# Stores of the first pass on GpSimd's queue, grouped matmuls, and half-size temporaries in an attention and two-MoE kernel

## The chip, the core and the metric

The kernel runs on one core of one Trainium2 chip. The metric is the time of one execution on the device in microseconds (us). Before the change three runs took 1383.2, 1383.8 and 1381.34 us, a median of 1383.2. All rows below are of one profiled execution of 1381.88 us.

The core has five engines with their own instruction rows: TensorE (PE, its weight loads shown as PEld), VectorE (DVE), ScalarE (ACT), GpSimd (POOL) and SyncE (SP). An engine takes its instructions in the order in which they are written and waits at each until its inputs and its output buffer are ready. A transfer (DMA) is an instruction of the engine that starts it; it then runs by itself.

## The reference

Attention between x (8 batches, 8 heads, 512 positions, 64 wide) and a state (32 positions), in both directions; the result is 4352 tokens of width 512. Two MoE layers follow, each with one weight pair 512 x 2048 and 2048 x 512, the first with a squared ReLU, the second with SiLU.

```
scores  = scale * x @ state^T;   xread = softmax(scores) @ state
scores2 = scale * state @ x^T;   sread = softmax(scores2) @ x
x = concat(xread, sread) as 4352 tokens of 512
h = relu(x @ w_in);  x = (h * h) @ w_out
h = x @ w_in2;       out = (h * sigmoid(h)) @ w_out2
```

## The kernel before

**Numbers.** Every product is made from pairs: a value is split into hi and lo in fp32r and three (in the last product two, the second on half the width) matmuls are added up. The weights come as 64-bit words and are converted on the chip: a transfer brings the raw words of a block into a page, ScalarE takes a first step (c_abs), VectorE three or four more (c_bits, c_sum or c_split).

**Buffers.** Nearly all data lie in 50 pages of 128 x 1024 fp32 and 10 quads of 128 x 512 (pools of rotating buffers). The eight banks of PSUM are four pairs: psA, psB, psC, psD.

**Stages.** The first layer does not multiply x by w1 for the part that comes from the state: it forms G = state x w1 (g_unit, line 579), four small 64 x 64 matmuls in fp32 for a group, two groups for a unit, 16 units in two halves. A group writes two banks; each bank is copied out into a page go (by ScalarE or VectorE), and from there some parts go to other pages (Glo) through small transfers, the rest to DRAM (g_d) and back later. The converted w1 is also stored (w1_store, line 604). Then the first pass runs: gemm1 into psC, ScalarE and VectorE make the squared ReLU (rg, gact), gemm2 adds into psA and psB. The scores of the attention (scores, line 641) go into psD between those. For each token block evac_a (line 820) writes sums of the result to DRAM (x_d). The second layer is two products (gemm3, gemm4) that each use seven half-size products in place of eight, with temporaries U, R, W and X in gemm4 (line 1034): U is copied from psA by ScalarE, then VectorE adds a bank to it block by block, and join (line 1060) adds the two halves of a temporary into the result z.

**The order.** A planner (class Plan) records all operations with what they read and write, gives each an urgency, and lists them in order per engine by modelled costs (cost, line 107; record, 142; urgency, 190; order, 220). An operation recorded with `either` may go to one of two engines; arith (line 451) chooses between VectorE and GpSimd, copy (line 455) between ScalarE and VectorE. All instructions are issued by one helper in record, so the profile shows line 186 for all of them (188 in the changed kernel); the buffers' names tell them apart. Before the change every transfer is SyncE's, through 8 lanes.

Of the kernel before, what the change touches and what calls it, by code (L numbers as in the profile page):

```python
# [27 lines left out]
class Plan:  # L28
# [6 lines left out]
    LATENCY = dict(act=dict(act=153, dve=147, pool=159, pe=265, dma=0),  # L35
                   dve=dict(act=128, dve=127, pool=155, pe=256, dma=0),
                   pool=dict(act=150, dve=150, pool=150, pe=309, dma=0),
                   pe=dict(act=197, dve=196, pool=200, pe=3, dma=0),
                   dma=dict(act=0, dve=0, pool=0, pe=100, dma=0))
    LANES = 8  # L40
    WINDOW = 25
# [9 lines left out]
    def __init__(self, bufs):  # L51
        self.bufs = bufs
        self.ops = []
        self.tiles = {}
        self.seen = {}
        self.slot = 0

# [49 lines left out]
    def cost(self, eng, method, writes, reads, args):  # L107
        size = 1
        for ap in writes + reads:
            n = 1  # L110
# [4 lines left out]
        if eng == "dma":  # L115
            n = 1
            for d in writes[0].shape:
                n *= d
            return n * 4 / 360
        if eng == "pe":  # L120
            n = 1
            for d in writes[0].shape[1:]:
                n *= d
            if method == "transpose":
                return 109

            share = 128 * 128 // (reads[0].shape[0] * writes[0].shape[0]) if args.get("tile_position") else 1
            return max(n / 2.4 + 13, 109) * (4 if args["rhs"].dtype == F32 else 1) / share
# [13 lines left out]
    def record(self, calls):  # L142
# [45 lines left out]
        self.ops.append(dict(forms=forms, deps=deps, uses=uses, slot=self.slot, port=port))  # L188

    def urgency(self, when=None):  # L190
# [3 lines left out]
        for i, o in enumerate(ops):  # L194
            if o["forms"][0][0] == "dma":
                cost[i] += self.LEAD
        late, t = [], 0.0
        for i, o in enumerate(ops):
            if o["forms"][0][0] == "pe":
                t = when[i] + cost[i] if when else t + cost[i]  # L200
                late.append(t)
            else:
                late.append(t + (self.DSLACK if o["forms"][0][0] == "dma" else self.SLACK))
# [16 lines left out]
    def order(self, when=None):  # L220
# [26 lines left out]
        ready = {e: [] for e in now}  # L247
# [8 lines left out]
        lanes, hw, wire = [], 0.0, 0.0  # L256
        port = dict(dve=0.0, pool=0.0)
        head = 0
        busy, warm = deque(), False

# [3 lines left out]
        def earliest(i, eng):  # L264
            o = ops[i]
            e = now[eng]
# [16 lines left out]
            if eng == "dma":  # L283
                e = max(e, hw)
                if len(lanes) >= self.LANES:
                    e = max(e, lanes[-self.LANES])
# [3 lines left out]
        while done < n:  # L290
# [4 lines left out]
            for eng, cand in ready.items():  # L295
                mine = []
                low = None
                for _, i in cand[:60]:
                    if ops[i]["slot"] > limit:
                        continue  # L300
                    e = earliest(i, eng)
# [8 lines left out]
                    if e <= now[eng] + self.PATIENCE[eng]:  # L310
                        break
                for e, i in mine:
                    if e <= low + self.PATIENCE[eng]:
# [16 lines left out]
            if eng == "pe":  # L330
# [4 lines left out]
                end[i] = now[eng] = e + cost * (1 if warm else 2)  # L335
                if busy and e - busy[-1][1] < 10:
                    busy[-1][1] = end[i]
# [12 lines left out]
            for t in o["uses"]:  # L350
                users_left[t] -= 1
                seems = e + self.DMA_SEEMS if eng == "dma" else end[i]
# [10 lines left out]
    def best(self):  # L363
        when, found = None, None
        for _ in range(self.ROUNDS):
# [12 lines left out]
def attn_moe_moe_kernel(  # L378
# [35 lines left out]
    T, D = plan.engine("pe", nc.tensor), plan.engine("dma", nc.sync)  # L414
# [115 lines left out]
    def c_store(key, dst):  # L530
        D.dma_start(dst, cv[key].rearrange("p (k n) -> p k n", k=2))
# [47 lines left out]
    def g_unit(i):  # L579
# [61 lines left out]
    def scores(b, g):  # L641
# [178 lines left out]
    def evac_a(s, j, n):  # L820
# [16 lines left out]
        for i in SEQ:  # L837
            at(s + 1, "dma", lambda i=i: D.dma_start(x_d[(i, j)].rearrange("(k p) n -> p k n", p=P), v[SRC_B[i]]))
# [195 lines left out]
    def gemm4(q):  # L1034
# [40 lines left out]
        U = new("U4")  # L1075
        for b in range(c):
            A.copy(U[:, b], BA[b])
# [14 lines left out]
        X = new("X4")  # L1092
# [143 lines left out]
    base = A_END + 2  # L1236
    for u in range(NU):
# [60 lines left out]
```

## Time and profile before

| | |
|---|---|
| runs | 1383.2, 1383.8, 1381.34 us |
| profiled execution | 1381.88 us, span 1380.1 us, mean granted clock 0.996 |
| PE busy | 1335.8 us, 97% of the span, 6892 matmuls |
| DVE busy | 1056.3 us, 77%, 1598 instructions |
| ACT busy | 701.0 us, 51%, 1080 instructions |
| POOL busy | 48.9 us, 4%, 41 instructions |
| DMA | 283.08 MB, mean 205 GB/s, one queue at 61.4% of 16 engines |

The share of an engine is a mean over the whole span and hides the stages: the first 100 us are conversion of weights and the first half of G, 140 to 160 us hold the second half of G, 160 to 960 us the first pass and gemm3, the rest ends with gemm4. A row of a timeline has the start, the duration of the row's instructions together (x2, x8 count them), and in brackets how long the engine was idle just before and what ended that.

### The profile page before, as it was taken

The numbers are of one execution on the slowest core, as the hardware profiler recorded it, in microseconds if no ns is written. First come the engines' busy times: TensorE is split into PE (matmuls) and PEld (weight loads), VectorE is DVE, ScalarE is ACT, GpSimd is POOL, SyncE is SP. The second block draws the span as 40 slices with busy tenths as digits, with TensorE's granted clock in tenths as the row PEclk, the third lists the DMA queues.
The fourth block names the chain that finished last, engine by engine and source line by source line (L and its number), as shares of the span: only waits on it lengthen the run. The fifth ranks groups of instructions, "written<-read, shape, count | busy, mean of one in ns | idle before, by whom it ended". The sixth has DMA issues, their size and how long they took to land. (4 is left out here: it accounts for less than half of the span.)

```text
span 1380.1 us, 19261 instructions
## 1 busy us (share of the span) xinstructions
PE 1335.8 (97%) x6892; PEld 1107.9 (80%) x6892; DVE 1056.3 (77%) x1598; ACT 701.0 (51%) x1080; POOL 48.9 (4%) x41
## 2 busy tenths in 40 slices
PE   5889999999999999999999999999998999999998
PEld 1457588888888888888988888999787888888887
DVE  6979488878898888875898866777887676665664
ACT  5755776555555646554662434244455444344442
POOL 0000001110000000000020000000111000000000
PEclk9999999999999999999999999999999999999999
DMA  8761764436264546342759956667899666665663
GB/s 302 262 244 62 223 219 131 123 120 216 80 198 127 168 144 194 112 153 107 225 177 328 363 208 233 248 233 255 280 338 362 195 215 231 220 204 187 201 205 114
DMA packets 206959, 283.08 MB, mean 205 GB/s; under 512 B 13456, under 2 KB 148112, under 8 KB 206864
## 3 DMA queue, kind: packets, MB, share of 16 engines
q1 hardware_dynamic: 206864, 281.86, 61.4%
q8 instruction: 54, 0.88, 0.3%
q14 instruction: 41, 0.34, 0.1%
HBM read 161.35 MB, written 116.26 MB: 201 GB/s over the span
## 5 line engine op out<-in xcount | busy, mean ns | idle before, releaser
L186 ACT ACTIVATE rg<-psC 128x512 f32<-128x512 f32 (+1 forms) x144 | 82.6, 574 | 199.0 <-PE psC L186 195.6
L186 PE MATMUL psC<-AThi,Ghi 128*128 128x512 f32 x256 | 101.6, 400 | 6.0 <-ACT rg L186 3.1
L186 DVE TENSOR_TENSOR gact<-rg,gact 128x512 fp32r<-128x512 f32 (+1 forms) x139 | 90.9, 656 | 19.0 <-ACT rg L186 12.8
L186 PE MATMUL psC<-ATlo,Ghi 128*128 128x512 f32 x256 | 101.1, 398 | 2.2 <-DVE ATlo L186 2.2
L186 PE MATMUL psC<-AThi,Glo 128*128 128x512 f32 x256 | 101.1, 399 | 1.7 <-DVE Glo L186 1.7
L186 ACT ACTIVATE gact<-rg 128x512 fp32r<-128x512 f32 (+1 forms) x144 | 87.7, 609 | 6.9 <-DMA g<-go 3.4
L186 DVE TENSOR_TENSOR rg<-rg 128x512 f32<-128x512 f32 (+1 forms) x66 | 43.7, 662 | 48.4 <-ACT rg L186 48.0
L186 PEld LDWEIGHTS psC<-AThi,Ghi 128*128 128x128 f32 x256 | 48.1, 188 | 21.4 <-ACT AThi L186 4.6
L186 DVE TENSOR_TENSOR W<-psD,U 128x512 f32<-128x512 f32 (+2 forms) x57 | 35.4, 631 | 35.9 <-PE psD L186 35.8
L186 PEld LDWEIGHTS psC<-AThi,Glo 128*128 128x128 f32 x256 | 48.0, 188 | 16.2 <-issue 3.3
L186 PEld LDWEIGHTS psC<-ATlo,Ghi 128*128 128x128 f32 x256 | 48.2, 189 | 14.8 <-DVE ATlo L186 2.9
L186 ACT ACTIVATE r<-r 128x1024 f32<-128x1024 f32 (+2 forms) x20 | 18.6, 932 | 73.3 <-DVE r L186 61.8
L186 DVE TENSOR_SCALAR cv<-cv 128x1024 f32<-128x1024 f32 (+1 forms) x64 | 43.4, 686 | 8.2 <-ACT cv L186 7.9
L186 ACT ACTIVATE rg<-rg 128x512 f32<-128x512 f32 (+1 forms) x78 | 46.3, 594 | 0.0
L186 DVE TENSOR_TENSOR U<-psB,U 128x512 f32<-128x512 f32 (+2 forms) x57 | 35.0, 629 | 14.1 <-PE psB L186 12.6
L186 DVE TENSOR_TENSOR W<-psC,U 128x512 f32<-128x512 f32 (+2 forms) x40 | 24.2, 609 | 27.6 <-PE psC L186 27.2
L186 ACT ACTIVATE cv<-raw 128x512 f32<-128x512 f32 x64 | 40.7, 668 | 8.9 <-DMA raw<-in_w_dram 8.9
L186 PE MATMUL psA<-cc,st 64*64 64x512 f32 x128 | 25.9, 641 | 17.7 <-DVE cc L186 17.3
L186 DVE SCALAR_TENSOR_TENSOR cc<-raw,cv 128x512 int32<-128x512 int32 x64 | 41.9, 684 | 1.4 <-DMA g<-go 1.2
L186 DVE SCALAR_TENSOR_TENSOR cv<-raw,cv 128x512 f32<-128x512 uint32 x64 | 41.5, 682 | 0.2
L186 DVE TENSOR_TENSOR Glo<-Glo,Ghi 128x1024 fp32r<-128x1024 f32 x31 | 37.7, 1216 | 1.2 <-ACT Ghi L186 1.0
L186 ACT COPY U<-psA 128x512 f32<-128x512 f32 (+2 forms) x57 | 28.9, 538 | 14.9 <-PE psA L186 14.3
(1244 smaller groups left out, 4276.2 us busy)
## 6 DMA issues: line engine op xcount, KB each, us to landing
raw<-in_w_dram SPq DMA_DIRECT2D x64, 512.0 KB, 6.4
t<-s SPq DMA_DIRECT2D x36, 512.0 KB, 5.0
Glo<-g SPq DMA_DIRECT2D x96, 128.0 KB, 4.6
t<-r SPq DMA_DIRECT2D x24, 512.0 KB, 4.6
xTr<-in_xT_dram SPq DMA_DIRECT2D x16, 512.0 KB, 8.3
g<-go SPq DMA_DIRECT2D x16, 512.0 KB, 5.7
xnr<-in_xN_dram SPq DMA_DIRECT2D x16, 512.0 KB, 5.6
x<-yt SPq DMA_DIRECT2D x32, 256.0 KB, 4.0
```

The source lines that it names most:

```text
L186: lambda engine=engine, method=method, a=a, k=k: getattr(engine, method)(*a, **k)))
```

## The change

Four parts. The stores c_store, w1_store, those of G to g_d and those of evac_a to x_d are started by GpSimd and not by SyncE: 119 transfers. The planner gets a second kind of transfer for them ("sdma"), on GpSimd's time with 1000 ns each. In the first pass arith goes to VectorE alone (18 operations that stood on GpSimd), and the bank copies of the first half of G go to ScalarE alone. The four matmuls of a group of G, or of a group of scores, are placed next to each other. In gemm4 U, R, W and X are quads, one for each block of 128 tokens, in place of pages for two blocks, and a join is made per block.

```diff
+    DMA = ("dma", "sdma")
     LANES = 8
+    ISSUE = 1000
     WINDOW = 25
...
-
-            share = 128 * 128 // (reads[0].shape[0] * writes[0].shape[0]) if args.get("tile_position") else 1
-            return max(n / 2.4 + 13, 109) * (4 if args["rhs"].dtype == F32 else 1) / share
+            return max(n / 2.4 + 13, 109) * (4 if args["rhs"].dtype == F32 else 1)
...
+            if o["group"] is not None:
+                cost[i] /= len(self.members[o["group"]])
...
+                    g = ops[i]["group"]
+                    if g is not None and i not in rest:
+                        if any(left[m] for m in self.members[g]):
+                            continue
+                        e = max(earliest(m, eng) for m in self.members[g])
+                    else:
...
-            elif eng == "dma":
-                hw = e + 450
-                now[eng] = e + 60
-                wire = max(wire, e + 1100) + cost
+            elif eng in self.DMA:
+                issue = 450 if eng == "dma" else self.ISSUE
+                hw[eng] = e + issue
+                now[clock[eng]] = e + (60 if eng == "dma" else issue)
+                wire = max(wire, e + 650 + issue) + cost
                 end[i] = wire + 1500
-                lanes.append(end[i])
+                lanes[eng].append(end[i])
...
-    T, D = plan.engine("pe", nc.tensor), plan.engine("dma", nc.sync)
+    T = plan.engine("pe", nc.tensor)
+
+    D, DS = plan.engine("dma", nc.sync), plan.engine("sdma", nc.gpsimd)
...
+    pool_stores = [True]
+
     def arith(op, o, a, b):
         kw = dict(out=o, in0=a, in1=b, op=op)
-        plan.either((V, "tensor_tensor", kw), (G, "tensor_tensor", kw))
+        if pool_stores[0]:
+            V.tensor_tensor(**kw)
+        else:
+            plan.either((V, "tensor_tensor", kw), (G, "tensor_tensor", kw))
 
...
-        D.dma_start(dst, cv[key].rearrange("p (k n) -> p k n", k=2))
+        DS.dma_start(dst, cv[key].rearrange("p (k n) -> p k n", k=2))
...
             ts = [acc_tile(bp), acc_tile(bp + 1)]
+            plan.together = ("G", i, bp)
             for k in range(2):
                 for r in range(2):
                     ps, co = slice(r * 64, (r + 1) * 64), 64 * (r ^ k)
                     T.matmul(out=ts[k][co:co + 64], lhsT=st[ps, bp + k, p].rearrange("p e n -> p (e n)"),
                              rhs=pg[ps], start=True, stop=True, tile_position=(r * 64, co))
+            plan.together = None
             o2 = page(f"go{i}{bp}", F32).rearrange("p (k f) -> p k f", k=2)
             for k in range(2):
-                copy(o2[:, k], ts[k])
+                (A.copy if 4 * q < PARTS[0][1] else copy)(o2[:, k], ts[k])
...
-                D.dma_start(g_d[q][0][p], o2[:, 1])
+                DS.dma_start(g_d[q][0][p], o2[:, 1])
             else:
-                D.dma_start(g_d[q][1][p], o2)
+                DS.dma_start(g_d[q][1][p], o2)
 
     def w1_store(i):
-        D.dma_start(w1_d[i], w1p.pop(("w1", i)))
+        DS.dma_start(w1_d[i], w1p.pop(("w1", i)))
 
...
+            plan.together = ("scores", b, g)
             for l in range(2):
                 for r in range(2):
                     h, ps = 2 * l + r, slice(r * 64, (r + 1) * 64)
                     T.matmul(out=t[h * NS:(h + 1) * NS], lhsT=st[ps, b // 2, 2 * g + l, b % 2],
                              rhs=x[ps, l * 512:(l + 1) * 512], start=True, stop=True, tile_position=(r * 64, h * NS))
+            plan.together = None
...
-            at(s + 1, "dma", lambda i=i: D.dma_start(x_d[(i, j)].rearrange("(k p) n -> p k n", p=P), v[SRC_B[i]]))
+            at(s + 1, "dma", lambda i=i: DS.dma_start(x_d[(i, j)].rearrange("(k p) n -> p k n", p=P), v[SRC_B[i]]))
...
 
+        def quads_of(name):
+            return [quad(f"{name}{b}") for b in range(c)]
+
         def add(o, banks, a):
             for b in range(c):
-                V.tensor_tensor(out=o[:, b], in0=banks[b], in1=a[:, b], op=ALU.add)
+                V.tensor_tensor(out=o[b], in0=banks[b], in1=a[b], op=ALU.add)
 
         def join(z, a):
-            arith(ALU.add, z, a[:, :, 0:256], a[:, :, 256:512])
+            for b in range(c):
+                arith(ALU.add, z[:, b], a[b][:, 0:256], a[b][:, 256:512])
 
...
         z = [new(f"z{t}") for t in range(2)]
         ls, hs = slice(0, 256), slice(256, 512)
         prod(1, BA, True, False)
-        U = new("U4")
+        U = quads_of("U4")
         for b in range(c):
-            A.copy(U[:, b], BA[b])
+            A.copy(U[b], BA[b])
         prod(6, BB, True, True)
         add(U, BB, U)
         prod(2, BA, False, True)
-        R = new("R4")
+        R = quads_of("R4")
         for b in range(c):
-            A.copy(R[:, b], BA[b])
+            A.copy(R[b], BA[b])
         join(z[0][:, :, ls], R)
         prod(7, BD, True, False)
-        W = new("W4")
+        W = quads_of("W4")
         add(W, BD, U)
         prod(5, BC, True, False)
         add(W, BC, W)
         join(z[1][:, :, hs], W)
         prod(4, BD, False, True)
-        X = new("X4")
+        X = quads_of("X4")
         add(X, BD, U)
         join(z[1][:, :, ls], X)
...
+    pool_stores[0] = False
...
```

The planner's order then differs at many places; three of them follow. TensorE's row where the scores of the first batch stand, before: psD are scores (four matmuls make a group), psC a product of the first layer, psA one of the second.

```order
L186 MATMUL psC_219<-AThi_277,Ghi_298 128x512
L186 MATMUL psD_221<-xTr_321,st 32x512
L186 MATMUL psC_219<-AThi_277,Glo_258 128x512
L186 MATMUL psD_221<-xTr_321,st 32x512
L186 MATMUL psC_219<-ATlo_278,Ghi_298 128x512
L186 MATMUL psD_221<-xTr_321,st 32x512
L186 MATMUL psC_219<-AThi_277,Ghi_298 128x512
L186 MATMUL psD_221<-xTr_321,st 32x512
L186 MATMUL psC_219<-AThi_277,Glo_258 128x512
L186 MATMUL psC_219<-ATlo_278,Ghi_298 128x512
L186 MATMUL psA_214<-gact,hi('w2', 2)_324 128x512
```

After the change, the same place:

```order
L188 MATMUL psC_219<-AThi_277,Ghi_298 128x512
L188 MATMUL psC_219<-AThi_277,Glo_258 128x512
L188 MATMUL psC_219<-ATlo_278,Ghi_298 128x512
L188 MATMUL psC_219<-AThi_277,Ghi_298 128x512
L188 MATMUL psC_219<-AThi_277,Glo_258 128x512
L188 MATMUL psC_219<-ATlo_278,Ghi_298 128x512
L188 MATMUL psD_221<-xTr_321,st 32x512 x4
L188 MATMUL psA_214<-gact,lo('w2', 2)_325 128x512
L188 MATMUL psA_215<-gact,lo('w2', 2)_325 128x512
```

The four psD matmuls stood one by one between psC matmuls; now they follow both psC products in one piece. VectorE's row in the conversion of the first weights, before (cv and cc are steps of the conversion, go is a page that takes G from a bank):

```order
L186 SCALAR_TENSOR_TENSOR cc<-raw,cv 128x512
L186 TENSOR_TENSOR cc<-cc,cv 128x1024
L186 SCALAR_TENSOR_TENSOR cc<-raw,cv 128x512
L186 TENSOR_SCALAR cv<-cv 128x1024
L186 TENSOR_SCALAR cv<-cc 128x1024
L186 COPY go_249<-psB_216 128x512
L186 SCALAR_TENSOR_TENSOR cv<-raw,cv 128x512 x2
L186 TENSOR_SCALAR cv<-cv 128x1024
L186 TENSOR_TENSOR cc<-cc,cv 128x1024
```

and after:

```order
L188 SCALAR_TENSOR_TENSOR cc<-raw,cv 128x512
L188 TENSOR_TENSOR cc<-cc,cv 128x1024
L188 SCALAR_TENSOR_TENSOR cc<-raw,cv 128x512
L188 TENSOR_SCALAR cv<-cv 128x1024
L188 TENSOR_SCALAR cv<-cc 128x1024
L188 TENSOR_SCALAR cv<-cv 128x1024
L188 SCALAR_TENSOR_TENSOR cv<-raw,cv 128x512 x2
L188 SCALAR_TENSOR_TENSOR cc<-raw,cv 128x512
L188 TENSOR_TENSOR cc<-cc,cv 128x1024
```

The copy out of psB is gone from this place, and a step of a later block stands there. SyncE's row in the first half of G, before (g are stores of G, w1d of w1, raw are loads of weights, xTr loads of x):

```order
L186 DMA g_207<-go_249 128x1024
L186 DMA g_207<-go_251 128x1024
L186 DMA w1d_101<-cc 128x1024
L186 DMA raw<-in_w_dram 128x1024 x2
L186 DMA g_208<-go_257 128x512
L186 DMA raw<-in_w_dram 128x1024 x2
L186 DMA xTr_321<-in_xT_dram 128x2x512
L186 DMA g_209<-go_260 128x1024
L186 DMA g_208<-go_261 128x512
L186 DMA xTr_332<-in_xT_dram 128x2x512
L186 DMA raw<-in_w_dram 128x1024 x3
L186 DMA g_209<-go_262 128x1024
```

GpSimd's row after, from its first store on:

```order
L188 DMA w1d_100<-cc 128x1024
L188 DMA g_206<-go_239 128x512
L188 DMA g_207<-go_242 128x1024
L188 DMA w1d_101<-cc 128x1024
L188 DMA g_206<-go_243 128x512
L188 DMA g_207<-go_244 128x1024
L188 DMA g_206<-go_248 128x512
L188 DMA g_207<-go_249 128x1024
```

Stores and loads stood in one row; now the stores have GpSimd's row from the first on, behind its two MEMSETs, and the loads keep SyncE's.

## Rows read from the trace of the kernel before

**Rows 1.** Stretches: start:end, us, then PE, PEld, DVE, ACT, POOL busy (x instructions), PEclk, DMA share, GB/s
```profile
20.00:48.00 28.00, 23.33 (x136) 5.38 (x128) 21.04 (x37) 20.47 (x39) 0.00 (x0) 1.00 0.65 203
48.00:100.00 52.00, 42.13 (x156) 28.01 (x157) 43.72 (x66) 32.41 (x55) 1.25 (x2) 0.94 0.81 291
100.00:140.00 40.00, 37.68 (x165) 29.72 (x164) 38.51 (x64) 21.40 (x39) 0.00 (x0) 1.00 0.13 53
140.00:160.00 20.00, 20.00 (x138) 6.79 (x138) 5.44 (x8) 15.41 (x29) 0.00 (x0) 1.00 0.66 201
160.00:960.00 800.00, 799.74 (x4058) 687.65 (x4057) 645.30 (x1074) 418.19 (x689) 30.71 (x23) 1.00 0.58 190
960.00:1380.00 420.00, 407.77 (x2225) 348.78 (x2223) 289.61 (x333) 184.75 (x222) 14.46 (x8) 1.00 0.70 231
```

**Rows 2.** Timeline of VectorE: start, us, engine, line, operation, [idle before <-releaser]
```profile
27.61 0.69 DVE L186 COPY go<-psB 128x512 f32<-128x512 f32 x1 [5.66 <-PE psB L186]
...
51.54 1.23 DVE L186 TENSOR_TENSOR cc<-cc,hi('w2', 0)_295 128x1024 f32<-128x1024 f32 x1 [1.05 <-ACT hi('w2', 0)_295 L186]
...
74.77 1.23 DVE L186 TENSOR_TENSOR cc<-cc,hi('w2', 2)_324 128x1024 f32<-128x1024 f32 x1 [4.20 <-ACT hi('w2', 2)_324 L186]
...
82.97 0.69 DVE L186 TENSOR_REDUCE sm<-U 128x16 f32<-128x512 f32 x1 [2.84 <-ACT U L186]
```

**Rows 3.** Timeline of ScalarE, 20 to 85 us
```profile
26.69 1.07 ACT L186 COPY go<-psA 128x512 f32<-128x512 f32 x2 [0.83 <-PE psA L186]
...
60.49 0.60 ACT L186 ACTIVATE rg<-psC 128x512 f32<-128x512 f32 x1 [1.28 <-DMA g<-go]
...
65.20 1.04 ACT L186 CAST Ghi<-Glo 128x1024 fp32r<-128x1024 f32 x1 [2.19 <-DMA w1d<-cc]
...
73.69 1.05 ACT L186 CAST hi('w2', 2)_324<-cc 128x1024 fp32r<-128x1024 f32 x1 [2.05 <-DMA g<-go]
...
79.09 0.60 ACT L186 ACTIVATE rg<-psC 128x512 f32<-128x512 f32 x1 [3.31 <-PE psC L186]
```

**Rows 4.** Timeline of SyncE's queue, 20 to 100 us
```profile
35.49 15.32 SPq L186 DMA_DIRECT2D Glo<-go  x22
50.85 3.94 SPq L186 DMA_DIRECT2D g<-go  x6
...
59.34 2.38 SPq L186 DMA_DIRECT2D raw<-in_w_dram  x2
```

**Rows 5.** Timeline of TensorE, at four places
```profile
48.01 0.73 PE L186 MATMUL psC<-AThi,Ghi 128*128 128x512 f32 x2 [1.68 <-ACT AThi L186]
...
96.78 0.63 PE L186 MATMUL psC<-AThi,Glo 128*128 128x512 f32 x1
97.21 0.63 PE L186 MATMUL psA<-gact,lo('w2', 3)_343 128*128 128x512 f32 x1
...
139.95 1.09 PE L186 MATMUL psA<-cc,st 64*64 64x512 f32 x8
140.86 1.02 PE L186 MATMUL psB<-cc,st 64*64 64x512 f32 x4
141.81 0.50 PE L186 MATMUL psC<-AThi,Ghi 128*128 128x512 f32 x1
...
158.85 0.50 PE L186 MATMUL psC<-AThi,Glo 128*128 128x512 f32 x1
```

**Rows 6.** Timeline of GpSimd at 225 us
```profile
225.06 1.30 POOL L186 TENSOR_TENSOR gact<-rg,gact 128x512 fp32r<-128x512 f32 x1 [135.42 <-ACT rg L186]
```

**Rows 7.** Timeline of VectorE at 225 to 240 us
```profile
225.79 0.85 DVE L186 TENSOR_SCALAR e<-e,sm 128x512 f32<-128x512 f32 x1
...
239.57 0.49 DVE L186 TENSOR_SCALAR e<-e,sm 128x512 f32<-128x512 f32 x1
```

**Rows 8.** Waits of TensorE, 1040 to 1360 us: engine and line waited for, us, times, longest
```profile
PE psD L186 <- DVE W L186: 1.9, 2, 1.3
PE psA L186 <- ACT U L186: 1.9, 4, 0.8
```

More of the change, by code (lines that the diff above doesn't have):

```diff
@@ L56, in __init__ @@
         self.slot = 0
+        self.together = None
     def tile(self, pool, shape, dt, tag, name, space="sb"):
@@ L114, in cost @@
         psum = any(self.tiles.get(ap.tensor.name, (0, 0, ""))[2] == "ps" for ap in writes + reads)
-        if eng == "dma":
+        if eng in self.DMA:
             n = 1
@@ L187, in record @@
         port = {c[0]: self.shares(c[0], writes, reads) for c in calls}
-        self.ops.append(dict(forms=forms, deps=deps, uses=uses, slot=self.slot, port=port))
+        self.ops.append(dict(forms=forms, deps=deps, uses=uses, slot=self.slot, port=port,
+                             group=self.together if eng == "pe" else None))
     def urgency(self, when=None):
@@ L194, in urgency @@
         for i, o in enumerate(ops):
-            if o["forms"][0][0] == "dma":
+            if o["forms"][0][0] in self.DMA:
                 cost[i] += self.LEAD
@@ L202, in urgency @@
             else:
-                late.append(t + (self.DSLACK if o["forms"][0][0] == "dma" else self.SLACK))
+                late.append(t + (self.DSLACK if o["forms"][0][0] in self.DMA else self.SLACK))
         before = [list(o["deps"]) for o in ops]
@@ L246, in order @@
         now = dict(pe=600.0, act=1900.0, dve=1070.0, pool=1150.0, dma=600.0)
-        ready = {e: [] for e in now}
+        clock = dict({e: e for e in now}, sdma="pool")
+        ready = {e: [] for e in clock}
         def add(i):
@@ L259, in order @@
         busy, warm = deque(), False
+        rest, begun = [], 0.0
         def fresh(i):
@@ L265, in earliest @@
             o = ops[i]
-            e = now[eng]
+            e = begun + 7 if i in rest else now[clock[eng]]
             for d in o["deps"]:
@@ L282, in earliest @@
                 e = max(e, port["pool" if eng == "dve" else "dve"])
[L283 to L286, printed above, removed]
+            if eng in self.DMA:
+                e = max(e, hw[eng])
+                if len(lanes[eng]) >= self.LANES:
+                    e = max(e, lanes[eng][-self.LANES])
             return e
@@ L297, in order @@
                 low = None
-                for _, i in cand[:60]:
-                    if ops[i]["slot"] > limit:
+                for _, i in [key[m] for m in rest] if eng == "pe" and rest else cand[:60]:
+                    if ops[i]["slot"] > limit and i not in rest:
                         continue
-                    e = earliest(i, eng)
+                    g = ops[i]["group"]
[4 more added lines that the diff above has]
+                    else:
+                        e = earliest(i, eng)
                     if e is None:
@@ L309, in order @@
                     low = e if low is None else min(low, e)
-                    if e <= now[eng] + self.PATIENCE[eng]:
+                    if e <= now[clock[eng]] + self.PATIENCE[clock[eng]]:
                         break
                 for e, i in mine:
-                    if e <= low + self.PATIENCE[eng]:
+                    if e <= low + self.PATIENCE[clock[eng]]:
                         if best is None or (e, key[i]) < best[:2]:
@@ L334, in order @@
                 warm = work > (1000 if warm else 2400)
-                end[i] = now[eng] = e + cost * (1 if warm else 2)
+                end[i] = e + cost * (1 if warm else 2)
+                now[eng] = max(now[eng], end[i])
+                if o["group"] is not None:
+                    rest, begun = [m for m in rest or self.members[o["group"]] if m != i], e
                 if busy and e - busy[-1][1] < 10:
-                    busy[-1][1] = end[i]
+                    busy[-1][1] = max(busy[-1][1], end[i])
                 else:
                     busy.append([e, end[i]])
-            elif eng == "dma":
-                hw = e + 450
-                now[eng] = e + 60
-                wire = max(wire, e + 1100) + cost
+            elif eng in self.DMA:
[3 more added lines that the diff above has]
+                wire = max(wire, e + 650 + issue) + cost
                 end[i] = wire + 1500
-                lanes.append(end[i])
+                lanes[eng].append(end[i])
             else:
@@ L351, in order @@
                 users_left[t] -= 1
-                seems = e + self.DMA_SEEMS if eng == "dma" else end[i]
+                seems = e + self.DMA_SEEMS if eng in self.DMA else end[i]
                 last_end[t] = max(last_end[t][0], seems), max(last_end[t][1], end[i])
@@ L364, in best @@
         when, found = None, None
+        self.members = defaultdict(list)
+        for i, o in enumerate(self.ops):
+            if o["group"] is not None:
+                self.members[o["group"]].append(i)
         for _ in range(self.ROUNDS):
```

13 lines of the change are left out of this document (7 added, 6 removed).

## The prediction

> **What bounds the kernel now.** I read the busy time of each engine in stretches first [rows 1]. From 160 to 960 us TensorE has work in 799.74 of 800 us: nothing to win there, only to lose. It idles in four places: 28 - 23.33 = 4.7 us at 20 to 48, 52 - 42.13 = 9.9 us at 48 to 100, 2.3 us at 100 to 140, and 12.2 us at 960 to 1380, of which the start of the last product and the tail are part. The stretch 140 to 160 is full but is slow in itself (below). The change touches all of these but the tail.
>
> Then I read VectorE's timeline from 20 to 100 us for its idle time, because the conversion of the weights runs there as one chain on that engine (21.04 of 28 us, then 43.72 of 52 us busy). Four waits hold nearly all of it [rows 2]: 5.66 us before a copy of G out of a bank (the copy stood in VectorE's row while its matmuls were not done), 1.05 and 4.20 us on ScalarE's casts, 2.84 us on U, which ScalarE writes. ScalarE's own waits say where those come from [rows 3]: 1.28, 2.19 and 2.05 us end on a store (g<-go, w1d<-cc), that is on a page that a store still holds, and 3.31 us end on TensorE's psC. Last, SyncE's issues [rows 4]: 22 small loads of Glo take its queue from 35.49 for 15.32 us, the stores of G follow from 50.85, the loads of the next raw weights from 59.34. So pages are freed late because stores stand in line behind loads.
>
> **The change part by part.** The profiled run is 1381.88 us with a span of 1380.1; it lies 1.3 us under the median of 1383.2. I sum against the profiled run.
>
> *A, to the first product at 48.01 [rows 5].* The copy that VectorE waits 5.66 us for goes to ScalarE, where 32 copies of the first half now stand for certain. VectorE gains the wait and the 0.69 us of the copy. Late next is ScalarE: 32 copies at 1.07 / 2 = 0.535 us [rows 3] are 17.1 us, beside casts, where it had 20.47 us busy in all of the 28 us from 20 to 48 and so 7.5 us to spare. Ends: VectorE's whole idle time there, 28 - 21.04 = 7.0 us, and 2 us if ScalarE takes up the rest. I take -5, near the row of the wait.
>
> *B, 48 to 100.* Stores leave SyncE's queue, so a page of G is released once its store is done, not after 15.32 us of loads; the raw loads move up as well. Of VectorE's waits, 1.05 + 4.20 are of this kind. The four matmuls of a group of scores no longer stand one by one between products, so U is done earlier and the 2.84 us goes as well. Together 8.1 us; what is late next is ScalarE, busy 32.41 of 52 us, and TensorE itself. A later wait always takes some of such a sum. I take -5, ends 0 and -8.1. The rows say that a place in the queue costs here: 15.32 / 22 = 0.70 us for each load ahead of a store. The Trainium skill ("DMA: Bandwidth & Descriptors", section "Issuing engines are not separate DMA queues") says that starting transfers on several engines saves only the sequencer's time to start them, usually small beside the transfer; by it B would be near 0 and the sum near 1375. The trace disagrees as far as the first row of SyncE's issues goes, since 15.32 us of sequencer are not small here; that GpSimd's are as quick to land, no run here shows.
>
> *The clock.* The granted clock at 48 to 100 is 0.94, and two matmuls at 96.78 and 97.21 start 0.43 us apart, the low level of the two (1.2 GHz) after TensorE had idled. A denser stretch may keep it high; worth at most 0.06 x 52 = 3.1 us. I take -0.5, since the idle time in front of it falls but does not vanish.
>
> *C, the second half of G.* From 139.95 to 158.85 is 18.9 us. A group takes 0.91 us (139.95 to 140.86), 16 groups 14.6. Of the 138 instructions there some 128 are of groups and 10 are products, each 0.22 us at full clock (half of the 0.43), together 2.2. About 2.1 us is left: a product inside a group leaves half a group behind that takes as long as a whole (140.86 to 141.81, 0.95 for x4). Kept together that goes. I take -1.5; ends -3, and +1 for one group that has to wait for both its banks while nothing else may enter.
>
> *D, 18 operations of GpSimd in the first pass go to VectorE.* Such a one takes 1.30 us on GpSimd [rows 6]; on VectorE a sum of 128x1024 takes 1.23 [rows 2], so one of 128x512 about 0.6, and 18 about 11 us. VectorE is busy 645.30 of 800 us there, and this covers them unless several stand before a matmul. +0.5, ends 0 and +3.
>
> *E, last product.* TensorE waits 1.9 us for ScalarE's U and 1.9 us for VectorE's W [rows 8]. With a buffer for each block of 128 tokens, the second copy or addition no longer holds back what needs only the first block, and four pages are free for loads. The joins are twice as many at half size; VectorE, busy 289.61 of 420 us, hides their fixed parts. With 10 half-size buffers and 8 in use, a block of the next product could wait for one. -2.5, ends 0 and -3.8.
>
> *F, what the stores cost on GpSimd.* No run here shows a DMA issued by it. What the trace shows is that an operation on GpSimd slows VectorE: the same operation took 0.85 us beside one [rows 6, 7], and 0.49 alone. In the stretch that VectorE paces there are 16 stores of g and 4 of w1d. Between nothing and 0.36 us each is 0 to 7 us; I take +2, nearer the lower end since a store is no arithmetic. Later stores fall where VectorE has room.
>
> Sum: -5 -5 -0.5 -1.5 +0.5 -2.5 +2 = -12, so 1381.9 - 12 = 1370.
>
> **The rivals.** *1. The stores come late from GpSimd.* Then pages are freed no earlier, B and the clock's half microsecond go, and the sum is -6.5: about 1375. For it: with only 50 pages, ScalarE already waits on stores; in the new order ScalarE and SyncE wait on GpSimd's stores too. Against it: GpSimd has nothing else to do at 20 to 100 (1.25 us busy). The Trainium skill ("SBUF — State Buffer", section "SBUF: two separate sides") says that a transfer issued by GpSimd has its descriptors written by that engine, and that it can't write them while VectorE runs certain two-port operations; VectorE is 84% busy there, so this would be such a lateness, and no run here shows it yet.
>
> *2. Slower: VectorE is held at each of GpSimd's stores.* Place: the weights' conversion up to about 85 us, where a microsecond of VectorE is one of the kernel. The longest price the rows allow is GpSimd's 1.30 us an operation; at 1 us the 20 stores cost 20. Without F's own +2 the sum is -14, so it comes out at +6, 1388 (1394 at 1.30). It decides from 14 / 20 = 0.7 us a store. For it: 0.85 against 0.49. Against it: that difference is 0.36, half the price needed.
>
> *3. No change: the gain of the first 100 us is given back.* From 100 to 140 VectorE is busy 38.51 of 40 us while TensorE waits 2.3: if that stretch is set by VectorE's work and not by when TensorE got there, A, B and C are only waited for later, and -2.5 of E stands against D's +0.5 and F's +2: about 1382. Against it: VectorE's chain itself moves forward with A and B, and its work after is no larger until D's operations.
>
> **How the numbers follow.** My forecast has 0.68, rival 1 0.15, rival 2 0.09, rival 3 0.08. Within 0.2%, about 2.8 us, counts as no change. Faster: 0.68 + 0.15 = 0.83; same 0.08; slower 0.09. All terms at their good ends (-7 -8.1 -3.1 -3 -3.8, D and F at 0) would give 1357, and they will not all be there; likely ones lie between 1361 and 1377. The range goes on to 1382 for rivals 1 and 3; rival 2 and the far good end stay out, not 2 in 10.
>
> **What would show it.** A: the 5.66 us before the copy is gone from VectorE, and the first product starts at about 43. B: the waits on casts of w2 are under 2 us together; stores are issued within a few microseconds of their copies; no wait on g<-go on ScalarE. C: 17 us or so from the first to the last group. D: from 160 to 960 TensorE stays under 2 us idle. E: no wait on U or W over 0.5 us. F: VectorE's conversions of the first stretch have the same mean as before. Wrong would be: stores that land late with ScalarE's waits now on them; VectorE's operations there longer by half; TensorE idle at 100 to 140 by as much as it came early; or new waits for half-size buffers after 960.

## The result and the profile after

The changed kernel takes 1362.45 us (median of four runs, 1361.81 to 1362.73) against 1383.5 us before in the same comparison: a ratio of 0.9848 with a 95% interval of 0.9831 to 0.9865. It is 21 us faster, inside the range (1361 to 1382) by 1.5 us at its fast end, where 1370 was forecast. The profiled execution took 1361.81 us with a span of 1360.0, 20.1 us less than that of before.

The stretches of the changed kernel, in the columns of [rows 1]:

```profile
20.00:48.00 28.00, 22.61 (x147) 8.15 (x144) 25.43 (x43) 22.79 (x44) 11.18 (x18) 0.94 1.03 406
48.00:100.00 52.00, 47.24 (x197) 35.38 (x196) 49.65 (x76) 36.62 (x63) 0.53 (x1) 0.93 0.57 180
100.00:140.00 40.00, 37.93 (x186) 25.01 (x185) 34.88 (x66) 23.43 (x44) 7.05 (x9) 0.96 0.33 117
140.00:160.00 20.00, 20.00 (x117) 11.10 (x114) 14.55 (x22) 10.34 (x19) 5.41 (x10) 1.00 0.95 366
160.00:960.00 800.00, 799.44 (x4053) 686.80 (x4052) 646.31 (x1073) 420.29 (x690) 71.37 (x88) 1.00 0.56 188
960.00:1360.00 400.00, 393.40 (x2174) 339.70 (x2172) 277.61 (x351) 178.18 (x212) 11.89 (x7) 1.00 0.71 233
```

VectorE is busy 25.43 of 28 us and 49.65 of 52 us, where it was 21.04 and 43.72. The transfers fill their engines from 20 to 48 us (share 1.03, 406 GB/s; before 0.65, 203), and TensorE's granted clock is lower at 20 to 48 and at 100 to 140, not higher. From 160 to 960 us TensorE and VectorE are busy as long as before.

Where the time went is read from landmarks on TensorE. In the changed kernel they are these (timeline; [rows 5] has the same places of before):

```profile
41.77 0.73 PE L188 MATMUL psC<-AThi,Ghi 128*128 128x512 f32 x2 [3.94 <-ACT Ghi L188]
...
69.91 1.93 PE L188 MATMUL psD<-xTr,st 64*32 64x512 f32 x8 [2.21 <-DMA xTr<-in_xT_dram]
...
128.59 1.09 PE L188 MATMUL psA<-cc,st 64*64 64x512 f32 x8
129.61 0.50 PE L188 MATMUL psC<-AThi,Glo 128*128 128x512 f32 x1
130.04 1.09 PE L188 MATMUL psB<-cc,st 64*64 64x512 f32 x8
...
150.82 0.50 PE L188 MATMUL psC<-AThi,Ghi 128*128 128x512 f32 x1
```

For the last product of the first layer, the row of its matmuls by tile (least/median/most ns, first and last start), before and after:

```profile
L186 PE MATMUL psC<-AThi,Glo x256: 389/389/628, 48.6 to 650.0; 128*128 128x512 f32 x128
```

```profile
L188 PE MATMUL psC<-AThi,Glo x256: 387/389/796, 43.0 to 637.7; 128*128 128x512 f32 x128
```

| stage | before | after | change | predicted |
|---|---|---|---|---|
| to the first product | 48.0 | 41.8 | -6.2 | A -5 |
| from there to the second half of G | 91.9 | 86.8 | -5.1 | B -5, clock -0.5, F +2 |
| from there to the last product of the first layer | 510.1 | 509.1 | -1.0 | C -1.5, D +0.5 |
| from there to the end of the span | 730.1 | 722.3 | -7.8 | E -2.5 |
| sum | 1380.1 | 1360.0 | -20.1 | -12 |

Of the 8.1 us that the forecast lacked, the last stage holds 5.3, the second 1.6 (F's 2 us did not come) and the first 1.2.

VectorE's larger waits up to 100 us, as in [rows 2]:

```profile
41.75 1.23 DVE L188 TENSOR_TENSOR Glo<-Glo,Ghi 128x1024 fp32r<-128x1024 f32 x1 [1.59 <-ACT Ghi L188]
...
53.23 1.22 DVE L188 TENSOR_TENSOR Glo<-Glo,Ghi 128x1024 fp32r<-128x1024 f32 x1 [1.36 <-ACT Ghi L188]
...
72.09 0.69 DVE L188 TENSOR_REDUCE sm<-U 128x16 f32<-128x512 f32 x1 [0.86 <-ACT U L188]
```

The waits of 5.66, 4.20 and 2.84 us are gone; the 1.59 us are new. ScalarE shows where that comes from, and SyncE's and GpSimd's issues what stands behind it:

```profile
40.68 1.04 ACT L188 CAST Ghi<-Glo 128x1024 fp32r<-128x1024 f32 x1 [1.92 <-DMA Glo<-go]
```

```profile
18.34 30.29 SPq L188 DMA_DIRECT2D Glo<-go  x16
48.72 2.24 SPq L188 DMA_DIRECT2D raw<-in_w_dram  x3
```

```profile
18.14 0.56 POOL L188 DMA_DIRECT2D g<-go  x1 [0.93 <-ACT go L188]
19.86 0.54 POOL L188 DMA_DIRECT2D g<-go  x1 [1.16 <-ACT go L188]
20.39 2.17 POOL L188 DMA_DIRECT2D w1d<-cc  x1
```

No wait on g<-go or w1d<-cc is left on ScalarE. A store is issued by GpSimd in about 0.55 us (three of those up to 140 us in 2.2 to 2.7; see F below). But the small transfers Glo<-go now land 7.5 us after their issue, where it was 2.1 (issues from 14 to 50 us: count, size, median us to landing; before, then after):

```profile
Glo<-go SPq DMA_DIRECT2D x31, 64.0 KB, 2.1
```

```profile
g<-go POOLq DMA_DIRECT2D x8, 512.0 KB, 8.5
...
Glo<-go SPq DMA_DIRECT2D x16, 64.0 KB, 7.5
```

### The profile page after: what moved, and what is told of

Same layout as the page of the kernel before. It is cut to its first block, busy times and chain, and to the rows that moved or that the text cites. A ratio compares the mean times of both kernels' runs of the same rounds, so it can differ in the third digit from the quotient of the medians.

```text
span 1360.0 us, 19397 instructions
## 1 busy us (share of the span) xinstructions
PE 1325.9 (97%) x6892; PEld 1107.7 (81%) x6892; DVE 1061.3 (78%) x1645; ACT 700.9 (52%) x1082; POOL 112.8 (8%) x143
## 5 line engine op out<-in xcount | busy, mean ns | idle before, releaser
L188 DVE TENSOR_TENSOR gact<-rg,gact 128x512 fp32r<-128x512 f32 (+1 forms) x144 | 94.2, 656 | 19.5 <-ACT rg L188 16.3
L188 DVE TENSOR_TENSOR rg<-rg 128x512 f32<-128x512 f32 (+1 forms) x59 | 38.6, 654 | 49.8 <-ACT rg L188 49.5
L188 ACT ACTIVATE rg<-rg 128x512 f32<-128x512 f32 (+1 forms) x85 | 50.9, 599 | 0.0
L188 POOL DMA_DIRECT2D x<-y x27 | 19.3, 716 | 207.8 <-DVE y L188 68.5
```

The source lines that it names most:

```text
L188: lambda engine=engine, method=method, a=a, k=k: getattr(engine, method)(*a, **k)))
```

## The experiments

Each part alone, on the kernel before; then parts undone in the changed kernel; then the disputed costs. All times are medians, with the ratio to the kernel before run beside them. That kernel's own median was 1382.0 to 1383.5 us beside these runs, so a difference of under 2 us between two of them can't be told. Every edit also gives the planner another order, so a run shows a part together with the order that comes with it; grp_only and no_grp change the modelled cost of the small matmuls as well. The four parts alone gave 8.5, 4.6, 5.3 and 0.8 us, 19.2 together, of the changed kernel's 21.

**q_only**, the quads alone:

```diff
-        U = new("U4")
+        U = quads_of("U4")
...
-            arith(ALU.add, z, a[:, :, 0:256], a[:, :, 256:512])
+            for b in range(c):
+                arith(ALU.add, z[:, b], a[b][:, 0:256], a[b][:, 256:512])
...
```

> The kernel before with the half-size temporaries of the last product alone. Theory: the gain after the first pass is this part's own. In the kernel before TensorE waits there 3.3 us for U, 1.9 for W and 1.4 for loads of g070, and smaller waits add up; with them gone the time is 7 to 8 us shorter, about 1375.5, and up to 960 us nothing changes. Rival: the waits go because the other parts free pages and move the loads, and the buffers give only what was predicted, 2.5 us: about 1381.

Measured 1374.4 us, ratio 0.9936 (0.9917 to 0.9954): 8.5 us, the theory's side. In its profile the last product of the first layer starts at 650.7 us, no earlier than before, and the rest of the span is 1373.5 - 650.7 = 722.8 us (before 730.1, after 722.3). The gain of the last stage belongs to this part. TensorE's waits from 960 us on, before and then here:

```profile
PE psA L186 <- ACT U L186: 3.3, 6, 0.9
PE psD L186 <- DVE W L186: 1.9, 2, 1.3
PE psD L186 <- ACT g070hi L186: 0.9, 1, 0.9
PE psD L186 <- DVE g070lo L186: 0.5, 1, 0.5
```

```profile
PE psA L186 <- ACT U L186: 0.9, 1, 0.9
PE psC L186 <- DVE W L186: 0.2, 1, 0.2
```

6.6 us of waits are 1.1. The loads of g070 were waits too. Of the 7.3 us of this stage that makes 5.5; where the other 1.8 lie, no row singles out.

**st_only**, the stores of the first pass on GpSimd, with its arithmetic on VectorE:

```diff
-        D.dma_start(w1_d[i], w1p.pop(("w1", i)))
+        DS.dma_start(w1_d[i], w1p.pop(("w1", i)))
...
```

> The kernel before with the stores of the first pass on GpSimd (and the arithmetic of that pass on VectorE alone), nothing else. Theory: stores waiting behind loads held the pages, so most of the gain of the first 140 us is theirs: 6 to 9 us shorter, about 1375, with ScalarE's waits on g<-go and w1d<-cc under 1 us together; the 5.66 us of VectorE before its copy may stay. Rival: the row of VectorE with that copy, and the split scores, were what cost, and stores alone give 0 to 3 us: 1380 to 1383.

Measured 1378.34 us, ratio 0.9964 (0.9951 to 0.9977): 4.6 us. That is between the two numbers. VectorE waits there as follows:

```profile
27.20 0.69 DVE L190 COPY go<-psB 128x512 f32<-128x512 f32 x1 [5.86 <-PE psB L190]
...
68.93 1.22 DVE L190 TENSOR_TENSOR cc<-cc,hi('w2', 2)_324 128x1024 f32<-128x1024 f32 x1 [1.16 <-ACT hi('w2', 2)_324 L190]
```

The wait on pages fell from 4.20 to 1.16 us; the one before the copy stayed. The second half of G starts at 133.1 us, 6.8 earlier than before. Some 2.6 us of that are given back behind the first layer (732.7 us from its last product on, before 730.1). TensorE's waits there are 6.6 us as before, so what gives them back is open.

**grp_only**, the matmuls of a group together:

```diff
+            plan.together = ("G", i, bp)
             for k in range(2):
...
+            plan.together = None
...
```

> The kernel before with the four matmuls of a group kept together, nothing else. Theory: the 2.84 us on U goes, and the second half of G gains about half a microsecond: 1 to 4 us shorter, about 1380.5. Rival: with groups, a product has to wait for a whole group and the second half pays as many changes between kinds as before: no difference, 1383.

Measured 1377.64 us, ratio 0.9956 (0.994 to 0.9973): 5.3 us, more than either said. It takes the wait before the copy, which the stores leave, and leaves or makes others:

```profile
48.37 1.23 DVE L188 TENSOR_TENSOR cc<-cc,hi('w2', 0)_295 128x1024 f32<-128x1024 f32 x1 [4.45 <-ACT hi('w2', 0)_295 L188]
...
74.98 1.22 DVE L188 TENSOR_TENSOR lo('w2', 2)_325<-cc,cv 128x1024 fp32r<-128x1024 f32 x1 [3.71 <-DMA g<-go]
```

No wait before a copy over 1.1 us and none on U, but 3.71 us on a page that a store holds, and 4.45 us on a cast of ScalarE that stood behind one that waited 4.84 us for Glo<-go. The first product starts 8.6 us earlier than before, the largest step of any part alone:

```profile
39.42 0.73 PE L188 MATMUL psC<-AThi,Ghi 128*128 128x512 f32 x2 [0.40 <-DMA Glo<-go]
```

**cp_only**, the copies of the first half on ScalarE:

```diff
-                copy(o2[:, k], ts[k])
+                (A.copy if 4 * q < PARTS[0][1] else copy)(o2[:, k], ts[k])
```

> The kernel before with the copies of the first half of G on ScalarE alone, nothing else. Theory: the 5.66 us before VectorE's copy goes and the first product starts 3 to 5 us earlier; half of it is lost again between 48 and 100 us, where pages are still held by late stores: 2 to 4 us shorter, about 1380. Rival: the stores decide when pages are free, the first product starts no earlier, and nothing is gained: 1383.

Measured 1382.12 us, ratio 0.9993 (0.9982 to 1.0003): no difference that can be told. The first product starts at 45.2 us, 2.9 earlier than before, but the wait did not go, it moved:

```profile
39.62 1.28 DVE L186 TENSOR_REDUCE sm<-U 128x16 f32<-128x512 f32 x2 [6.82 <-ACT U L186]
```

VectorE, without its copy in the way, went on for 11 us and then waited 6.82 us for U, the exponentials of the scores, which ScalarE makes. The matmuls of these scores were not what was late: VectorE had taken them from their bank by 27.4 us and had its own part of U ready at 32.1. ScalarE came to U only behind nine copies of G in its row:

```profile
38.94 1.17 ACT L186 ACTIVATE U<-U 128x512 f32<-128x512 f32 x2
```

**no_grp**, the changed kernel without the groups:

```diff
-            plan.together = ("G", i, bp)
+            plan.together = None
...
+            share = 128 * 128 // (reads[0].shape[0] * writes[0].shape[0]) if args.get("tile_position") else 1
...
```

> The changed kernel without the grouping of matmuls. Theory: it was the grouping, more than the copies on ScalarE, that took away VectorE's wait before its copy, since the group's matmuls stood one by one between scores; the first product falls back from 41.8 to 44 us or later, and the kernel loses what the part gained alone, 4 to 6 us: about 1367.5. Rival: with the copies on ScalarE and the stores on GpSimd nothing waits for a split group, and it loses 0 to 1 us: 1362 to 1363.5.

Measured 1368.34 us, ratio 0.989 (0.9875 to 0.9905): 5.9 us slower than the changed kernel's 1362.45, the theory's side. The first product starts at 46.0 us, and the wait of cp_only is back at the same place, with ScalarE at U from 39.25 us on:

```profile
39.95 1.28 DVE L190 TENSOR_REDUCE sm<-U 128x16 f32<-128x512 f32 x2 [6.90 <-ACT U L190]
```

**no_st**, the stores back on SyncE:

```diff
-        DS.dma_start(w1_d[i], w1p.pop(("w1", i)))
+        D.dma_start(w1_d[i], w1p.pop(("w1", i)))
...
```

> The changed kernel with its stores back on SyncE, all else kept. Theory: the stores gain what they gained alone, 4.5 us, and a little more since the denser start holds more pages: 1367 to 1369, with ScalarE's waits on g<-go and w1d<-cc back. Rival: grouping and copies had already taken the waits that stores make, and it loses under 2 us: 1362.5 to 1364.

Measured 1366.25 us, ratio 0.9878 (0.9861 to 0.9894): 3.8 us slower than the changed kernel, nearer to the theory and under its range. A wait on a store is back on VectorE (2.16 us on g<-go at 70.6 us). Its first product starts at 38.6 us, 3.2 earlier than in the faster kernel, and Glo<-go lands in 2.9 us.

**q_pages**, a half page in place of a quad:

```diff
-            return [quad(f"{name}{b}") for b in range(c)]
+            return [page(f"{name}{b}", F32)[:, :512] for b in range(c)]
```

> The changed kernel in which the temporaries of the last product are one for each block as now, but each in half of a page of its own: eight pages where there were four, and no quads. Theory: what helps is that a block no longer waits for the other one's operation; TensorE's waits on U and W stay under 1.5 us in the last product, and the time stays at 1362 to 1364. Rival: what helps is the pages that the quads set free for loads; with eight pages taken the waits for loads come back, larger than the 1.4 us of before, and the time is 1366 to 1371.

Measured 1367.56 us, ratio 0.9884 (0.987 to 0.9899): 5.1 us slower than the changed kernel, the rival's side. From 960 us on:

```profile
PE psA L188 <- ACT U L188: 2.9, 5, 0.9
PE psD L188 <- ACT g070hi L188: 1.4, 1, 1.4
```

The waits on W are gone, so those were the coupling of two blocks in one buffer; those on U and on the load stay, so those were pages. But this run takes eight pages where the kernel before took four, so its 5.1 us are what eight pages cost; the four that the quads set free are worth at most that, and how much is not shown.

**no_w1s**, no early stores of w1:

```diff
-        DS.dma_start(w1_d[i], w1p.pop(("w1", i)))
+        pg = w1p.pop(("w1", i))
+        if i >= PARTS[0][1] // 2:
+            DS.dma_start(w1_d[i], pg)
...
```

> The changed kernel without the four stores of w1 in the first half (512 KB each, 2.1 MB of the 14.1 MB that move between 14 and 50 us); the later loads read the blocks of the second half in their place, so part of the first layer is computed with other weights. Theory: with stores and loads in two queues the transfers fill the DMA engines from 14 to 48 us, the small loads of Glo take 7.5 us to land where they took 2.1, and the first product waits 3.9 us for them; with fewer bytes they land in 6 us or less and the first product starts 1.5 to 3 us sooner, at 39 to 40.3 us, and the time falls by 1 to 3 us, to about 1360.5. Rival: Glo is late because its row on SyncE waits for the copies and raw loads ahead, not for bytes; the first product stays at 41.5 or later and the time within 1 us of 1362.4.

Measured 1365.68 us, ratio 0.9878 (0.9857 to 0.9899): 3.2 us slower than the changed kernel. Half of the theory held: Glo<-go landed in 6.5 us (6 or less was expected), and the first product started at 39.6 us, 2.2 sooner. The half on the time failed, and the rival's time with it. Behind the early start the planner's order was another one: ScalarE waits 4.1 us on raw loads from 40 to 50 us (2.8 us the longest), TensorE 2.9 us on rg, and the second half of G starts at 131.5 us instead of 128.6. How much is the order and how much the bytes, this run can't tell.

**no_cp**, copies of the first half on either engine again:

```diff
-                (A.copy if 4 * q < PARTS[0][1] else copy)(o2[:, k], ts[k])
+                copy(o2[:, k], ts[k])
```

> The changed kernel in which the copies of the first half of G may again go to ScalarE or VectorE. Theory: alone this part gave under 1 us, and with groups kept together no copy stands long in VectorE's row; the time is within 1.5 us of the changed kernel, 1361 to 1364. Rival: VectorE sets the pace of the first 100 us, and each of its 0.69 us copies is paid: with a dozen of them 4 us or more are lost, 1366 or longer.

Measured 1363.15 us, ratio 0.9866 (0.9841 to 0.9892): 0.7 us from the changed kernel by the times and 2.5 by the ratios, no difference that can be told: the theory.

**arith_either**, the first pass's arithmetic on either engine again:

```diff
-    pool_stores = [True]
+    pool_stores = [False]
```

> The changed kernel in which the arithmetic of the first pass may again go to GpSimd. Theory: VectorE had room for the 18 operations, so no more than 1 us changes: 1361.5 to 1363.5. Rival: GpSimd's operations stand in its row ahead of stores and hold pages, and the stores come late: 1 to 4 us slower, about 1365.

Measured 1362.25 us, ratio 0.9859 (0.9838 to 0.988): not to be told from the changed kernel, the theory.

**issue550**, another cost in the planner:

```diff
-    ISSUE = 1000
+    ISSUE = 550
```

> The changed kernel, where the planner costs a store on GpSimd with 550 ns and not 1000. The trace has 0.53 to 0.56 us for most of them. Theory: the planner places stores and what waits for them nearer to what the chip does, and the 3.9 us before the first product and the 2.2 us on a load of x shrink: 1 to 4 us faster than the changed kernel, about 1360. Rival: the order shifts at random places, within 1 us either way: 1361.5 to 1363.5.

Measured 1363.63 us, ratio 0.9855 (0.9841 to 0.987): no gain, about the rival's bound. TensorE waits 2.7 us for Glo<-go before the first product, in place of 3.9, and the second half of G starts at 128.6 us all the same.

**gact_pool**, VectorE's work to idle GpSimd:

```diff
-        arith(ALU.subtract, pg[:, 512:512 + n], gq[:, :n], pg[:, :n].bitcast(F32))
+        if plan.slot < 14:
+            G.tensor_tensor(out=pg[:, 512:512 + n], in0=gq[:, :n], in1=pg[:, :n].bitcast(F32), op=ALU.subtract)
```

> The changed kernel with one operation of the first 14 steps of the first layer (gact = rg - gact, 128x512) moved from VectorE to GpSimd, which does nothing from 44 to 98 us. Theory: from 20 us to the second half of G VectorE has 102.5 us of work in every kernel run so far, and the stretch is that plus its idle time (6.1 us in the changed kernel); 14 operations of 0.68 us less are 9.5 us less work, of which the shared use of memory takes back 14 x 0.36 = 5: the stretch is 3 to 5 us shorter, and the time about 1358.5. Rival: what VectorE loses beside GpSimd's 1.3 us operations, and gact coming 0.6 us later each, takes all of it: VectorE's work stays at 100 or its idle time grows by as much, and the time is 1361.5 to 1365.

Measured 1366.83 us, ratio 0.9877 (0.9861 to 0.9894): 4.4 us slower than the changed kernel, beyond the rival's range too. VectorE's operations from 48 to 100 us (count, busy, mean ns), in the changed kernel and here:

```profile
L188 DVE SCALAR_TENSOR_TENSOR cc<-raw,cv 128x512 int32<-128x512 int32 x10 | 6.4, 682 | 0.0
...
L188 DVE TENSOR_SCALAR cv<-cc 128x1024 int32<-128x1024 int32 x5 | 3.3, 676 | 0.0
```

```profile
L188 DVE SCALAR_TENSOR_TENSOR cc<-raw,cv 128x512 int32<-128x512 int32 x10 | 9.7, 1016 | 0.0
...
L188 DVE TENSOR_SCALAR cv<-cc 128x1024 int32<-128x1024 int32 x5 | 5.5, 1109 | 0.0
```

VectorE has 13 operations fewer up to the second half and is busy longer (106.3 us where 102.5): in these two groups an operation took half as long again or more in the mean, some of them beside GpSimd.

**What the runs say together.** From 20 us to the second half of G, VectorE's busy time is nearly a constant of the work. The windows of that stretch, columns as in [rows 1], for before, after, cp_only, grp_only and st_only:

```profile
20.00:139.95 119.95, 103.08 (x453) 63.05 (x445) 103.27 (x165) 74.23 (x131) 1.25 (x2) 0.97 0.55 191
```

```profile
20.00:128.59 108.59, 96.37 (x450) 64.64 (x446) 102.48 (x166) 73.31 (x132) 15.51 (x22) 0.94 0.59 210
```

```profile
20.00:138.49 118.49, 101.99 (x455) 64.86 (x452) 101.83 (x163) 74.97 (x133) 1.25 (x2) 0.94 0.55 193
```

```profile
20.00:135.35 115.35, 96.92 (x452) 64.98 (x446) 102.97 (x165) 72.66 (x130) 1.56 (x2) 0.93 0.56 198
```

```profile
20.00:133.11 113.11, 97.95 (x448) 62.67 (x443) 102.69 (x166) 73.56 (x131) 13.49 (x22) 0.97 0.57 203
```

| kernel | stretch | VectorE busy | VectorE idle |
|---|---|---|---|
| before | 119.95 | 103.27 | 16.7 |
| cp_only | 118.49 | 101.83 | 16.7 |
| grp_only | 115.35 | 102.97 | 12.4 |
| no_grp | 114.45 | 102.16 | 12.3 |
| st_only | 113.11 | 102.69 | 10.4 |
| no_st | 111.91 | 102.45 | 9.5 |
| after | 108.59 | 102.48 | 6.1 |

The gain of the stretch is VectorE's idle time, 16.7 - 6.1 = 10.6 of 11.4 us. Of it the stores alone take away 6.3, the groups alone 4.3, the copies none, and the two add up to the 10.6. That they add up so exactly is in part luck: undone in the changed kernel, the stores give back 3.4 and the groups 6.2. And that VectorE's work is a floor under the stretch is argued from this table, not shown: no run took much work off VectorE, since gact_pool, which meant to, made it longer.

## Why the prediction was right in its sign and short in its size

*A, first product: -6.2 against -5, but by another cause.* The step that failed is "the copy that VectorE waits 5.66 us for goes to ScalarE ... VectorE gains the wait". The copies alone gave nothing measurable, since VectorE then waited 6.82 us for U; with the groups split again it waited 6.90 us with the copies still on ScalarE. So "late next is ScalarE" held where the groups were split, for the whole sum and not for a part of it. The cause that A left out is that matmuls of G and of the scores stood one by one. In the kernel before, one group of G with scores (psD) in it:

```profile
21.60 1.07 PE L186 MATMUL psB<-cc,st 64*64 64x512 f32 x4
22.61 1.04 PE L186 MATMUL psD<-xTr,st 64*32 64x512 f32 x2
23.58 1.08 PE L186 MATMUL psB<-cc,st 64*64 64x512 f32 x4
```

It takes 3.0 us, until the next row at 24.59, where an undivided one takes 0.91 [rows 5]. With groups whole, the first product starts at 39.4 us (grp_only) and 38.6 us (no_st); in the changed kernel it starts at 41.8 us, since late next there is the Glo transfer, in a stretch whose DMA engines are now full. That 9.4 us gained by the rest less 3.2 lost with the stores come near the term is luck.

*B: right in its larger part.* The stores' place in SyncE's row held the pages; the row's 15.32 us [rows 4] were the cost that the mechanism said. Of the two parts of B the waits on pages went with the stores (st_only). The 2.84 us on U, which B put down to the groups, went with any part: there is no such wait in grp_only, but 0.72 us in st_only and 0.79 in cp_only as well. The Trainium skill ("DMA: Bandwidth & Descriptors", section "Issuing engines are not separate DMA queues") says that another issuing engine saves only the sequencer's time; here that time was what the pages waited for, and st_only is 4.6 us faster by it. The same section's statement that all transfers end on the same 16 DMA engines agrees with the trace: share 1.03 from 20 to 48 us, and small transfers landing in 7.5 us instead of 2.1.

*The clock: wrong sign.* The granted clock of 20 to 48 and 100 to 140 us fell to 0.94 and 0.96 from 1.00, after TensorE had idled 3.9 us before the first product and 2.1 us before a product of w2. What that cost is not shown; if VectorE sets the pace there, little.

*C: right in kind, 0.9 of 1.5 us.* From the first group of the second half to the last product of the first layer every run with the groups takes 509.1 to 509.2 us and every run without them 509.9 to 510.1. But the second half of G itself is no shorter. From 128.59 to 150.82 us there are 16 groups, 19 products and three small transposes, before from 139.95 to 158.85 us 16 groups and 4 products. Less 0.22 us for each product, that is 18.1 and 18.0 us. The step that failed is "10 are products": the 138 instructions were counted up to 160 us, and the stretch up to 158.85 holds 4, so that 18.9 - 14.6 - 0.9 = 3.4 us hung on products inside groups and not 2.1. The changed kernel pays as much in another way. A group with one product behind it takes 130.04 - 128.59 = 1.45 us, against 0.91 + 0.22, and there are ten such places where there were four. The Trainium skill ("TensorEngine Tiling (Array Packing)", section "Key Properties") says that a change of the tiling mode drains TensorE; the 0.3 us, for the change there and back, agree with it. Where in the stage the 0.9 us arise is open.

*D: right in kind, and nothing of the 0.5 us.* Its cover held: VectorE is busy 646.31 of 800 us, arith_either is no faster, and in st_only, with this arithmetic on VectorE and no groups, the stage takes 510.0 us as before. That C and D together come out at the forecast -1 is luck.

*E: mechanism right, size wrong, the largest miss.* -7.8 against -2.5, and beyond the far end of -3.8. The step that failed is the end "-3.8". It was made of two rows of a window from 1040 us on: from 960 us on the waits were 6.6 us, with loads of g070 among them, and 1.2 are left. By q_pages up to 5 of the 8 us hang on the pages, which the prediction named and did not price. The 2.4 us of the stage that are not waits of TensorE stay open.

*F: nothing on VectorE.* VectorE's conversions take what they took: 0.683 us for cc<-raw from 14 to 85 us with 20 stores issued by GpSimd in that stretch (0.687 before). Rival 2's price is not there, and a GpSimd operation on data ([rows 6, 7], gact_pool) was the wrong neighbour to price it by.

Rival 1 was half there: the stores land late (8.5 us) but ScalarE waits for none of them. The Trainium skill ("SBUF — State Buffer", section "SBUF: two separate sides") says that GpSimd can't write the descriptors of such transfers while VectorE runs certain two-port operations. The trace agrees as far as the issue goes. Of GpSimd and VectorE in the changed kernel:

```profile
100.32 2.74 POOL L188 DMA_DIRECT2D w1d<-cc  x1 [0.60 <-DVE cc L188]
```

```profile
100.44 2.49 DVE L188 TENSOR_SCALAR cv<-cv 128x1024 f32<-128x1024 f32 x4
```

The issue ends 0.13 us after the last of the four TENSOR_SCALAR. The other two that take over 2 us, at 15.01 and 20.39 us, end 0.12 us after three such operations. But this is not what makes the 8.5 us. From 98 to 118 us, where VectorE has no gap and the DMA engines are mostly idle, GpSimd's stores land in 3.1 us in the median; in the kernel before, stores from SyncE took 9.0 us when the engines were full (72 to 88 us, share 1.03). Issues from 98 to 118 us after, then from 72 to 90 us before:

```profile
w1d<-cc POOLq DMA_DIRECT2D x4, 512.0 KB, 3.1
```

```profile
g<-go SPq DMA_DIRECT2D x2, 512.0 KB, 9.0
Glo<-g SPq DMA_DIRECT2D x8, 128.0 KB, 6.4
```

Rival 3 was wrong because VectorE's work did not set the stretch alone; its waits did as well.

## What to carry to other kernels

Where one engine seems to pace a stretch, take its busy time as fixed and count its idle time, by what it waits for: here that was the gain to be had, whichever engine started first. A wait that is taken away at one instruction is only gone if the thing waited for comes earlier; if the instruction is moved to another engine, what stands behind it in that engine's row comes late. And when buffers are set free, price the loads that they let in, over the whole stretch and not the two largest rows.

## What the runs showed of the hardware that was not expected

A store issued by GpSimd took 0.53 to 0.56 us of it and slowed VectorE by nothing that the rows show. The other way round VectorE held the store: three issues that began beside a run of TENSOR_SCALAR took 2.2 to 2.7 us and ended 0.12 to 0.13 us after it. A GpSimd operation on data beside VectorE took VectorE's operations from 0.68 to 1.02 and 1.11 us in the mean. The DMA engines were full at about 400 GB/s with two queues (406, 20 to 48 us after) and with one (412, 72 to 88 us before); a small transfer issued between large ones then took 7.5 us (64 KB, after) and 6.4 us (128 KB, before), where 64 KB took 2.1 us at a share of 0.65.
